# One head's exponential in seven units on GpSimd, in the forward attention of an adaLN transformer block

## The chip, the cores and the metric

The kernel runs on one core of one Trainium2 chip. The metric is the device time of one execution in microseconds (us). A core has five engines that run side by side and meet at semaphores: TensorE (PE, matrix products into PSUM), VectorE (DVE), ScalarE (ACT, here the exponentials), GpSimd (POOL) and SyncE (SP, which only issues DMAs). Each engine works through its own queue in order.

## The reference

The reference computes the output of one transformer block and all its gradients. The block has adaptive layer norms (shift, scale and gate from `silu(c) @ w_mod`), attention with 32 heads of 16 columns over 2048 tokens of width 512, and a squared-ReLU MLP of width 1792. All in bf16. The part that matters here is the attention of the forward pass:

```python
scores = jnp.einsum('bhqd,bhkd->bhqk', q, k) * Dh ** (-0.5)
p = _softmax(scores, axis=-1)
o = jnp.einsum('bhqk,bhkd->bhqd', p, v)
```

```python
h = _layernorm(x) * (1 + ca) + sa
x = x + ga * _A_ref(h, A_wqkv, A_wo)
...
_out, _vjp = jax.vjp(_f, A_x, A_wqkv, A_wo, B_w1, B_b1, B_w2, B_b2, c, w_mod)
```

## The kernel before

The kernel has four stages: a preparation (norm, first projections), the forward attention with the MLP and its gradients worked in between, the backward attention, and a tail of weight gradients. The change touches the forward attention alone.

**Units.** The forward attention is cut into 512 units `u`: four chunks of 512 queries (`qc`), in each of them eight head groups of four heads (`hg`), in each of them 16 tiles of 128 keys (`kt`). In the first query chunk unit `u` is key tile `u % 16` of head group `u // 16`. The loop runs `fscore(u)`, then `fpv(u - 2)`, then what is planned for unit `u`.

**Scores and exponentials.** `fscore` (L603 to L614) works in two pairs of heads. For each pair PE makes the scores of two heads, 128 keys by 512 queries each, in a PSUM tile `psST` of two banks; a row of `q` carries a bound on the row's maximum, so that no maximum has to be taken. ACT then takes the exponential of both heads at once, 1024 columns, into half of the SBUF tile `ET`, with the factor 0.25 of the scores in the same instruction (L614). There are three `psST` buffers, so 1.5 units.

**Products with V.** `fpv` (L616 to L630) multiplies the four heads' `ET` with `vaug` (V with a column of ones) into four row blocks of one PSUM tile `oacc`, which collects the 16 key tiles of a head group. At the last one DVE copies it to `ostage` (L632) and POOL casts that to `obf` (L640).

**Side work of the first chunk.** The remaining projections of the first stage are spread over its units by `plan_tasks`, an order written out by hand: key and query tiles (`key_tile`, L1050; `query_tile`, L1067; PE projects, DVE copies from PSUM, DVE squares the copy in `square`, L863), norms of them (`key_norm`: PE at L860, DVE's maximum at L857), an inverse square root in steps on DVE (`query_bound`, L1082 to L1093), rows of the modulation (L895, L897), columns of it (L885 to L888) and tiles turned to tokens (L1115, L1118, L1123). In units 83 to 110 DVE also normalizes and modulates tiles of x (L752 to L754), and from 113 on it forms gated gradients (L310). All PE products of this side work go through one PSUM buffer `pm` (pool `mm`, one buffer), which DVE empties. In a unit with no side product PE runs two products with zeros (`steady`, L657).

**POOL's queue.** POOL issues the row loads of the next head group (`fload`, `row_load`, L591): four of K rows, four of Q rows and one of the bounds, in the order of the program behind the `obf` cast of the last group. It also adds up row sums (`rowsum`, L168).

The queues of all engines are in program order (`manual_schedule`); the tile layer adds the semaphores.

Of the kernel before, what the change touches and what calls it, by code (L numbers as in the profile page):

```python
# [14 lines left out]
AF = mybir.ActivationFunctionType  # L15
ALU = mybir.AluOpType
AX = mybir.AxisListType
BF = dt.bfloat16
F32 = dt.float32

P = 128
# [3 lines left out]
DH = 16  # L25
HG = 8
FF = 1792
FC = 14
SCALE = 0.25
EPS = 1e-5  # L30
QPAD = 528


@with_exitstack
def kernel(
# [17 lines left out]
    PE = nc.tensor  # L53
    DVE = nc.vector
    ACT = nc.scalar
    POOL = nc.gpsimd
    SP = nc.sync

    persist = ctx.enter_context(tc.tile_pool(name="persist", bufs=1))
# [9 lines left out]
    DVE.memset(zeros[:], 0.0)  # L69
    onesf = persist.tile([P, 4], F32, name="onesf")  # L70
    DVE.memset(onesf[:], 1.0)
    modbc = persist.tile([P, 6, D], BF, name="modbc")
    modcol = persist.tile([P, 6, DC], F32, name="modcol")
    mean1 = persist.tile([P, TT], F32, name="mean1")
# [42 lines left out]
    def rsqrt_cols(pool, out, var, w):  # L117
        v, y, t = (pool.tile([P, w], F32, name=f"rsq{i}", tag=f"rsq{i}") for i in range(3))
        DVE.tensor_scalar(v[:], var, EPS, None, ALU.add)
        yi = y[:].bitcast(I32)  # L120
# [20 lines left out]
    vaug = vaugpool.tile([P, TT, H + 1, DH + 1], BF, name="vaug")  # L141
# [3 lines left out]
    with ExitStack() as ph:  # L145
        wk = ph.enter_context(tc.tile_pool(name="phC", bufs=2))
        ffw = ph.enter_context(tc.tile_pool(name="ffw", bufs=1))
        cb = ph.enter_context(tc.tile_pool(name="phMc", bufs=1))
# [29 lines left out]
        def later(lag, f, *args):  # L178
            due.append((unit[0] + lag, f, args, True))
# [407 lines left out]
        funits = [(qc, hg, kt) for qc in range(QC) for hg in range(HG) for kt in range(TT)]  # L587
# [5 lines left out]
        def fload(qc, hg):  # L593
# [6 lines left out]
            run_due()  # L600
            fh[qc, hg] = (qt_sb, kt_sb)

        def fscore(u):  # L603
            qc, hg, kt = funits[u]
            qt_sb, kt_sb = fh[qc, hg]
            ET = ework.tile([P, 4, 512], BF, name="ET", tag="ET")
            fe[u] = ET
            for pair in range(2):
                ps = pools["s"].tile([P, 2, 512], F32, name="psST", tag="psST")
                for hi in range(2):  # L610
                    r = 32 * (2 * pair + hi)
                    PE.matmul(ps[:, hi, :], kt_sb[r:r + 32, kt * P:(kt + 1) * P], qt_sb[r:r + 32, :],  # L612
                              start=True, stop=True, tile_position=(r, 0))
                ACT.activation(ET[:, 2 * pair:2 * pair + 2, :], ps[:], AF.Exp, scale=SCALE)  # L614

        def fpv(u):  # L616
            qc, hg, kt = funits[u]
            if kt == 0:
                fcur["o"] = pools["o"].tile([P, 512], F32, name="oacc", tag="oacc")
                if hg == 0:  # L620
                    fcur["rr"] = ework.tile([H, 512], F32, name="rrows", tag="rrows", bufs=1)
                    fcur["ou"] = ework.tile([P, 4, HG, P], BF, name="O_un", tag="O_un", bufs=1)
            oacc = fcur["o"]
            ET = fe.pop(u)
            for hq in range(4):
                h = hg * 4 + hq
                lhsT = vaug[:, kt].rearrange("p h c -> p (h c)")[:, h * (DH + 1):h * (DH + 1) + 32]
                PE.matmul(oacc[32 * hq:32 * hq + 32, :], lhsT, ET[:, hq, :],  # L628
                          start=(kt == 0), stop=(kt == TT - 1), tile_position=(0, 32 * hq), skip_group_check=True)
            if kt == TT - 1:  # L630
                ostage = ework.tile([P, 512], F32, name="ostage", tag="ostage", bufs=1)
                DVE.tensor_copy(ostage[:], oacc[:])  # L632
                obf = ework.tile([P, 512], BF, name="obf", tag="obf", bufs=2)
                if u == NF - 1:
                    fcur["last"] = ostage
                    return
                if hg == HG - 1:
                    DVE.tensor_copy(obf[:], ostage[:])
                else:
                    POOL.tensor_copy(obf[:], ostage[:])  # L640
                for hq in range(4):
                    h = hg * 4 + hq
                    later(2, sp, fcur["rr"][h:h + 1, :], ostage[32 * hq + 16:32 * hq + 17, :])
                later(3, sp, fcur["ou"][:, :, hg, :], obf[:], True)
                if hg == HG - 1:
                    fdone.append((u + 7, qc, fcur["rr"], fcur["ou"]))
# [252 lines left out]
        def prep():  # L899
# [19 lines left out]
            ACT.activation(tiny0[:], onesf[:, 0:1], AF.Sqrt)  # L919
            DVE.memset(epsc, EPS)  # L920
            DVE.memset(kmx, 0.0)
# [293 lines left out]
        with ExitStack() as ph2:  # L1215
# [3 lines left out]
            with tc.manual_schedule(engines={PE.engine, ACT.engine, DVE.engine, SP.engine, POOL.engine}):  # L1219
                fh[0, 0] = (qts[0], kts[0])  # L1220
                for u in range(NF + 2):
                    unit[0] = u
                    run_due()
                    if u < NF:
                        if funits[u][2] == (10 if u < 7 * TT else 2) and u + TT < NF:
                            fload(*funits[u + TT][0:2])
                        fscore(u)
                    begins = TT <= u - 2 < NF and funits[u - 2][2] == 0
                    if 2 <= u and not begins:
                        fpv(u - 2)  # L1230
# [15 lines left out]
                    if begins:  # L1246
                        fpv(u - 2)
# [55 lines left out]
        def last_chunk(O_c, L, w1T):  # L1303
# [29 lines left out]
            for half in range(2):  # L1333
# [12 lines left out]
                sd = wk.tile([P, 2], F32, name="sd2", tag="sd2")  # L1346
                DVE.tensor_scalar(sd[:], mv4[:, tis[0]:tis[1] + 1, 1], EPS, None, ALU.add)
                ACT.activation(sd[:], sd[:], AF.Sqrt)
# [170 lines left out]
            def ks_loads():  # L1519
                keep["KS"] = kpool.tile([P, TT, QPAD], BF, name="KS_tok", tag="ks")  # L1520
                POOL.memset(keep["KS"][:, :, D:QPAD], 0.0)
                for i in range(4):
                    later(1 + i, sp, keep["KS"][:, 4 * i:4 * i + 4, 0:D], k_st[:, 4 * i:4 * i + 4, :])
# [108 lines left out]
    with ExitStack() as ph:  # L1632
# [113 lines left out]
        def keep_warm():  # L1746
            PE.matmul(cur["vk"][0:DH, :], KS_tok[:, 0, D:QPAD], dOs_tok[:, 0, :], start=False, stop=False,
                      tile_position=(0, 0), skip_group_check=True)
# [79 lines left out]
        if True:  # L1828
# [4 lines left out]
            for b in range(NU // 4):  # L1833
                toks, bank = order_t if on_pe(b - 1) else order_n
                for tok in toks:
                    c, i = tok[0], int(tok[1:] or 0)
# [41 lines left out]
            late = (("dq", 1), ("vk", 4), ("dq", 2), ("vk", 5), ("dq", 3))  # L1878
# [367 lines left out]
```

## Time and profile before

| what | value |
|---|---|
| median of 3 runs | 2461.73 us (2460.39 to 2462.99) |
| the profiled execution | 2457.34 us, span 2455.5 us |
| first exponential of unit 0, last of unit 511 | 36.8 us, 978.5 us |
| first query chunk, 36.8 to 272.0 us | ACT busy 235.2, PE 222.5, DVE 122.5, POOL 51.0 us |
| busy in the whole span | PE 94%, ACT 93%, DVE 75%, POOL 20% |
| POOL's sum of 128x512 f32 tiles (L168 with g_c) | 1157 ns in the first chunk |
| DVE's copy of 128x512 f32 from PSUM (L632) | 687 ns |

Times in the profile are from one execution, counted from the start of its span. A line such as `L614 ACT ACTIVATE ET<-psST 128x1024 bf16<-128x1024 f32 x227 | 208.6, 1453 | 0.0` names the source line, the engine, the operation, what it writes and reads with shapes, how many there are, then busy us and mean ns of one, and the engine's idle time just before them with what ended it. A timeline line has start and duration in us first. Durations of ACT overlap, since an instruction is counted from when it enters the engine.

### The profile page before, as it was taken

The page shows a single profiled execution, that of the slowest core. Times are in us where ns is not written, and L with a number is a line of the kernel's source. Part 1 is how long each engine was busy: PE and PEld are TensorE (multiplying, and loading weights), DVE is VectorE, ACT ScalarE, POOL GpSimd, SP SyncE. Part 2 cuts the span into 40 slices and gives each one's busy share as a digit, 9 for nine tenths or more (in the row PEclk, how much of TensorE's full clock was granted, in tenths as well). Part 3 has the DMA queues.
Part 4 walks back from the last instruction along what each step waited for, and adds up shares of the span by engine and source line. Part 5 has one row for each costly group of instructions (what it writes and reads, how often), then busy time and mean ns, then how long its engine had stood idle before and what let it go on. Part 6 is the DMA issues. An engine that isn't in the chain of part 4 may idle for free. (4 is left out here: it accounts for less than half of the span.)

```text
span 2455.5 us, 49791 instructions
## 1 busy us (share of the span) xinstructions
PE 2307.4 (94%) x18926; PEld 774.3 (32%) x18926; DVE 1847.8 (75%) x2443; ACT 2295.4 (93%) x3579; POOL 500.1 (20%) x684
## 2 busy tenths in 40 slices
PE   8999899989998999889999999999999999999998
PEld 3232232333233323433333333233323233322243
DVE  6655464456445645679999999999999899999984
ACT  8999999999999999539999999999999999999964
POOL 2111224314542443110111101111011110110112
PEclk9999999999999999989999999999999899999999
DMA  4568445627683857879999999999999999999998
GB/s 155 138 158 188 110 113 120 170 68 125 99 178 62 139 81 165 223 191 193 206 206 201 204 203 208 205 207 204 206 208 210 203 204 209 203 203 199 204 209 171
DMA packets 1200324, 426.67 MB, mean 174 GB/s; under 512 B 1080758, under 2 KB 1177140, under 8 KB 1199956
## 3 DMA queue, kind: packets, MB, share of 16 engines
q1 hardware_dynamic: 1154900, 367.44, 79.7%
q0 software_dynamic: 23472, 33.77, 8.5%
q10 hardware_dynamic: 21712, 22.27, 3.8%
q8 instruction: 149, 2.44, 0.4%
q14 instruction: 91, 0.75, 0.1%
HBM read 85.46 MB, written 68.95 MB: 63 GB/s over the span
## 5 line engine op out<-in xcount | busy, mean ns | idle before, releaser
L1724 DVE TENSOR_TENSOR dS_u<-psD_u,E_u 128x1024 bf16<-128x1024 f32 x1024 | 1186.1, 1219 | 69.8 <-PE psD_u L1722 24.5
L614 ACT ACTIVATE ET<-psST 128x1024 bf16<-128x1024 f32 x1024 | 940.0, 1319 | 3.3 <-PE psST L612 3.3
L1708 ACT ACTIVATE E_u<-psS_A 128x512 bf16<-128x512 f32 x768 | 515.3, 671 | 15.4 <-DMA out_dram<-xlast 12.7
L1708 ACT ACTIVATE E_u<-psS_B 128x512 bf16<-128x512 f32 x768 | 507.9, 661 | 9.6 <-PE psD_u L1722 5.4
L1722 PE MATMUL psD_u<-iv,ido 32*128 32x512 bf16 x2048 | 408.8, 387 | 0.0
L612 PE MATMUL psST<-qt_sb,kt_sb 32*128 32x512 bf16 x2048 | 318.0, 382 | 41.2 <-ACT ET L614 38.0
L1708 ACT ACTIVATE E_u<-psS_C 128x512 bf16<-128x512 f32 x512 | 336.6, 657 | 2.3 <-PE psS_B L1702 0.8
L1702 PE MATMUL psS_A<-ik,iq 32*128 32x512 bf16 x768 | 293.0, 381 | 16.2 <-ACT E_u L1708 5.9
L1702 PE MATMUL psS_B<-ik,iq 32*128 32x512 bf16 x768 | 294.4, 383 | 7.9 <-ACT E_u L1708 0.2
L1809 POOL TENSOR_TENSOR dQacc<-dQacc,dqtmp 128x512 f32<-128x512 f32 x64 | 81.2, 1269 | 846.3 <-ACT dqtmp L1804 846.3
L1702 PEld LDWEIGHTS <-iq 32*128 32x128 bf16 x2048 | 130.1, 91 | 315.8 <-issue 299.7
L1764 PE MATMUL accVK<-dS_u,qz 128*32 128x512 bf16 x2048 | 212.8, 390 | 0.2 <-DVE dS_u L1724 0.2
L628 PE MATMUL oacc<-ET,vaug 128*32 128x512 bf16 x2048 | 206.6, 391 | 3.3 <-DVE ostage L632 3.3
L1773 PE MATMUL accVK<-E_u,dOs_tok 128*16 128x512 bf16 x2048 | 202.5, 385 | 0.0
L1702 PE MATMUL psS_C<-ik,iq 32*128 32x512 bf16 x512 | 194.2, 379 | 4.3 <-ACT dqtmp L1804 0.2
L612 PEld LDWEIGHTS <-kt_sb 32*128 32x128 bf16 x2048 | 89.6, 91 | 314.5 <-issue 290.1
L1791 PE MATMUL dqacc<-dsT,KS_tok 128*32 128x512 bf16 x2048 | 146.7, 384 | 18.4 <-DMA dsT<-dS_u 5.4
L1868 ACT ACTIVATE dsT<-ptT 128x1024 bf16<-128x1024 bf16 x126 | 145.0, 1150 | 3.1 <-PE ptT L1754 2.9
L1722 PEld LDWEIGHTS <-ido 32*128 32x128 bf16 x2048 | 104.5, 91 | 102.0 <-issue 95.6
L1764 PEld LDWEIGHTS <-qz 128*32 128x32 bf16 x2048 | 58.4, 94 | 177.3 <-issue 162.3
L252 DVE COPY part<-pm 128x512 f32<-128x512 f32 (+2 forms) x105 | 64.4, 614 | 63.5 <-PE pm L234 61.5
L324 DVE CAST dsT<-pm 128x512 bf16<-128x512 f32 x56 | 38.7, 691 | 84.9 <-PE pm L322 84.8
(435 smaller groups left out, 2700.6 us busy)
## 6 DMA issues: line engine op xcount, KB each, us to landing
p_st<-part POOLq DMA_DIRECT2D x36, 256.0 KB, 4.3
kt_sb<-qkT_st POOLq DMA_DIRECT2D x124, 64.0 KB, 3.9
wA<-in_B_w_dram SPq DMA_DIRECT2D x28, 256.0 KB, 5.8
w_nat<-in_B_w_dram SPq DMA_DIRECT2D x21, 256.0 KB, 4.7
w2T<-w2T_st SPq DMA_DIRECT2D x21, 256.0 KB, 5.5
p_st<-part POOLq DMA_DIRECT2D x27, 192.0 KB, 5.0
p_st<-part SPq DMA_DIRECT2D x18, 256.0 KB, 2.3
part<-p_st SPq DMA_DIRECT2D x18, 256.0 KB, 4.9
```

The costliest lines, as they stand in the source:

```text
L612: PE.matmul(ps[:, hi, :], kt_sb[r:r + 32, kt * P:(kt + 1) * P], qt_sb[r:r + 32, :], start=True, stop=True, tile_position=(r, 0))
L614: ACT.activation(ET[:, 2 * pair:2 * pair + 2, :], ps[:], AF.Exp, scale=SCALE)
L628: PE.matmul(oacc[32 * hq:32 * hq + 32, :], lhsT, ET[:, hq, :], start=(kt == 0), stop=(kt == TT - 1), tile_position=(0, 32 * hq), skip_grou ...
L1702: PE.matmul(psS[:], st["q"][r:r + 32, qt * P:(qt + 1) * P], st["k"][r:r + 32, kc * 512:kc * 512 + 512], start=True, stop=True, tile_positi ...
L1708: ACT.activation(bst[u][0][:, hq, :], sst.pop((u, hq))[:], AF.Exp, scale=SCALE)
L1722: PE.matmul(psD[:, hi, :], st["do"][r:r + 32, qt * P:(qt + 1) * P], st["v"][r:r + 32, kc * 512:kc * 512 + 512], start=True, stop=True, til ...
L1724: DVE.tensor_tensor(dS_u[:, 2 * pair:2 * pair + 2, :], psD[:], E_u[:, 2 * pair:2 * pair + 2, :], ALU.mult)
L1764: PE.matmul(cur["vk"][32 * hq:32 * hq + 32, :], hst[hg]["qz"][:, qt, hq, :], bst[u][1][:, hq, :], start=(qt == 0), stop=False, tile_positi ...
L1773: PE.matmul(acc[32 * hq:32 * hq + DH, :], dOs_tok[:, qt, (hg * 4 + hq) * DH:(hg * 4 + hq + 1) * DH], E_u[:, hq, :], start=False, stop=(qt ...
L1791: PE.matmul(acc[32 * hq:32 * hq + 32, :], KS_tok[:, kc * 4 + kt, h * DH:h * DH + 32], tT[:, :, hq * 4 + kt, :], start=(kt == 0), stop=(kt ...
L1809: POOL.tensor_tensor(dst2, dst, tmp[:], ALU.add)
L1868: ACT.activation(dst, pt[:], AF.Identity)
```

## The change

In the first query chunk, unit `16 * hg + 2` of the head groups 1 to 7 (units 18, 34, 50, 66, 82, 98 and 114) is treated in another way. Of its second pair of heads ACT takes the exponential of one head only, 512 columns. DVE multiplies the other head's scores by 0.25 log2(e) and puts them in SBUF as f32 (`staged`), and POOL raises 2 to them (`Epool`, bf16). POOL does this in one instruction of 512 columns for groups 1 to 3, in two of 256 for groups 4 and 5, and in four of 128 for groups 6 and 7. The product of that head with V is taken out of its own unit and done in the unit with `kt == 14` of the same group. `staged` and `Epool` take buffers of the tag `tk`, which is otherwise first used after this chunk.

In the built program the staging copy waits for ACT's half exponential of the same unit. On POOL the power stands behind the `obf` cast and ahead of the row loads of the next group; in group 7 one of these loads is ahead of it. In that group the staging copy stands between the first and the second of the gated gradients on DVE.

```diff
+LOG2E = 1.4426950408889634
...
+    twos = persist.tile([P, 1], F32, name="twos")
+    DVE.memset(twos[:], 2.0)
...
+        pooled = {16 * hg + 2: 512 // (1, 1, 1, 1, 2, 2, 4, 4)[hg] for hg in range(1, HG)}
+        owed = []
+
+        def on_pool(u, ET, scores):
+            staged = cb.tile([P, 512], F32, name="staged", tag="tk", bufs=5)
+            DVE.tensor_scalar(staged[:], scores, SCALE * LOG2E, None, ALU.mult)
+            out = cb.tile([P, 512], BF, name="Epool", tag="tk", bufs=5)
+            w = pooled[u]
+            for lo in range(0, 512, w):
+                POOL.tensor_tensor(out[:, lo:lo + w], twos[:].to_broadcast([P, w]), staged[:, lo:lo + w], ALU.pow)
+            owed.append((u, out))
+
         def fscore(u):
...
-                ACT.activation(ET[:, 2 * pair:2 * pair + 2, :], ps[:], AF.Exp, scale=SCALE)
+                if pair == 1 and u in pooled:
+                    ACT.activation(ET[:, 2, :], ps[:, 0, :], AF.Exp, scale=SCALE)
+                    on_pool(u, ET, ps[:, 1, :])
+                else:
+                    ACT.activation(ET[:, 2 * pair:2 * pair + 2, :], ps[:], AF.Exp, scale=SCALE)
 
         def fpv(u):
...
-            for hq in range(4):
+            parts = [(kt, hq, ET[:, hq, :]) for hq in range(3 if u in pooled else 4)]
+            if kt == 14 and owed:
+                v, late = owed.pop(0)
+                parts.append((funits[v][2], 3, late[:]))
+            for k, hq, rhs in parts:
                 h = hg * 4 + hq
-                lhsT = vaug[:, kt].rearrange("p h c -> p (h c)")[:, h * (DH + 1):h * (DH + 1) + 32]
-                PE.matmul(oacc[32 * hq:32 * hq + 32, :], lhsT, ET[:, hq, :],
+                lhsT = vaug[:, k].rearrange("p h c -> p (h c)")[:, h * (DH + 1):h * (DH + 1) + 32]
+                PE.matmul(oacc[32 * hq:32 * hq + 32, :], lhsT, rhs,
                           start=(kt == 0), stop=(kt == TT - 1), tile_position=(0, 32 * hq), skip_group_check=True)
```

## The prediction

> **What bounds the kernel now.** I read the page first: ACT is busy 93% of the span, PE 94%, and nearly all of the forty slices read 9 for ACT. The table by stage then shows the first query chunk alone, and the grouped lines of that stretch show what ACT does there.
>
> ```profile
> PE 2307.4 (94%) x18926; PEld 774.3 (32%) x18926; DVE 1847.8 (75%) x2443; ACT 2295.4 (93%) x3579; POOL 500.1 (20%) x684
> ...
> core 0: us, PE busy (x) PEld busy (x) DVE busy (x) ACT busy (x) POOL busy (x), PEclk, DMA share, GB/s
> 36.80:272.00 235.20, 222.53 (x1567) 70.94 (x1565) 122.51 (x246) 235.20 (x259) 50.97 (x97) 1.00 0.66 165
> ...
> L614 ACT ACTIVATE ET<-psST 128x1024 bf16<-128x1024 f32 x227 | 208.6, 1453 | 0.0
> ```
>
> ACT is busy for all 235.20 us of the chunk, with no idle time before any exponential. Its 256 exponentials of 1024 columns start 0.9165 us apart (the 1453 ns mean counts queueing), from 36.75 us on. So unit u needs its scores by 36.75 + 1.833u, and whatever makes ACT wait here lengthens the span one for one. PE computes scores about one unit ahead, and that lead is the only cushion. POOL is nearly free, DVE half busy.
>
> The timelines of DVE and PE around unit 34, a unit that the change touches, show how PE hangs on DVE:
>
> ```profile
> 99.37 0.68 DVE L857 TENSOR_REDUCE small<-pm 32x1 f32<-32x512 f32 x1
> 101.89 0.69 DVE L1050 CAST KT<-pm 128x512 bf16<-128x512 f32 x1 [1.83 <-PE pm L853]
> 102.61 0.43 DVE L863 TENSOR_TENSOR sqK<-KT 128x512 bf16<-128x512 bf16 x1
> ...
> 100.81 1.04 PE L853 MATMUL pm<-h1T,wqkv_nat 128*128 128x512 bf16 x4
> 101.78 0.60 PE L612 MATMUL psST<-qt_sb,kt_sb 32*128 32x512 bf16 x4
> 102.31 0.40 PE L628 MATMUL oacc<-ET,vaug 128*32 128x512 bf16 x4
> 103.09 0.38 PE L860 MATMUL pm<-sqK,small 128*32 128x512 bf16 x1 [0.38 <-DVE sqK L863]
> 103.31 0.59 PE L657 MATMUL oacc<-identb,zeros 128*16 128x512 bf16 x2
> 103.83 0.40 PE L612 MATMUL psST<-qt_sb,kt_sb 32*128 32x512 bf16 x4
> ```
>
> There is one `pm` buffer. PE's next side product waits until DVE has emptied it, and the next scores stand behind that product in PE's queue.
>
> Last, what an operation of POOL does to DVE (timeline of the second chunk, then one line's durations):
>
> ```profile
> 404.75 1.20 POOL L168 TENSOR_TENSOR racc<-racc,prod 128x512 f32<-128x512 f32 x1
> ...
> 405.33 0.91 DVE L505 TENSOR_TENSOR uqb<-dxn,tqb 128x512 bf16<-128x512 bf16 x1
> ...
> L505 DVE TENSOR_TENSOR uqb<-dxn,tqb x12: 415/774/909, 373.9 to 878.4; 128x512 bf16<-128x512 bf16 x12
> ...
> L1067 DVE CAST sP<-pm x15: 691/692/692, 72.5 to 182.6; 128x512 bf16<-128x512 f32 x15
> ```
>
> A DVE product of two SBUF tiles takes 0.415 us alone and 0.91 us when POOL's two-input sum is running: it ends 0.28 us after POOL's (404.75 + 1.20 = 405.95; 406.24). Evacuations of PSUM (L1067) never vary. So the DVE product waits out POOL's whole instruction.
>
> **What is saved.** In seven units ACT's second exponential has 512 columns instead of 1024. Exponentials of 512 columns (L1708, backward) start 0.48 us apart in the timeline, so 0.9165 - 0.48 = 0.44 us each, 3.1 us for seven. No more can be gained.
>
> **What moves at no cost.** Seven P·V products of 32 rows go from their unit to the one with kt = 14; a group of four starts within 0.01 us, and the fifth there costs at most one 0.2 us slot, covered by the filler products (L657). DVE's seven copies of PSUM to f32 (0.69 us, as the ostage copy L632) are 5 us of a half-busy engine.
>
> **POOL's queue.** The power stands ahead of the next group's nine row loads (0.5 us each to issue, 3.9 us to land). For group 4 they are needed at 153.0 us (PE's first scores of unit 64), and the power would start near 130.7. It may last 153.0 - 130.7 - 4.5 - 3.9 = 14 us before loads are late. The fourth head's product, due some 24 us after, comes later still.
>
> **The new wait.** DVE's staging copy waits for ACT's half exponential of its own unit, not just for PE's scores; that is how the built program orders the two readers of the score tile. ACT is about a unit behind PE, and DVE is in order: everything DVE owes PE queues behind. Unit 34: the half exponential starts at 36.75 + 69 x 0.9165 = 99.99, is done 0.6 us later (shortest L1708 row 0.592), and staging ends at 101.3. The reduction that ran at 99.37 runs at 101.3 to 102.0; PE's projection slips from 100.81 to 102.0; the scores of unit 36 follow 0.97 later, at 103.0, ready 0.38 later, at 103.4. ACT wants them at 102.74 - 0.44 = 102.3: 1.1 us idle, more than the 0.44 saved. The same sum gives 1.0 for unit 18 (70.05 reduction to 72.0, projection 71.47 to 72.65), 1.1 for unit 50 (L1082 from 129.17 to 130.6), about 1.5 for 66 (the same chain), 1.9 for 82 (DVE full), 0.8 for 98, 0 for 114 (filler products only): 7.4 us.
>
> **The power itself.** No row of before has one. The nearest is POOL's f32 sum of the same shape, 1.20 us, one pass: the lower end. A power needs a logarithm, a product and an exponential; the kernel's own inverse root (L1088 to L1093) takes six DVE passes. Four to twelve passes of 1.2 us give 4.8 to 14.4 us, an estimate. I take 5 us for 512 columns, since the sum is the only row of this engine and kind, and keep 1.2 and 14 for the range. The Trainium skill (GPSIMD Engine Reference, section Elementwise — side-by-side cycle accounting) puts data-dependent branching at about 12 cycles an element, which would be 5.1 us here and leave the sum where it is; no run shows it yet.
>
> **The ports.** If POOL holds DVE out as in L505, a power of 5 us stops DVE's next two-SBUF-input operation, and all that is queued behind it. Unit 34: the power runs 101.4 to 106.4; the projection's cast ends at 103.8; its square (L863) waits and ends at 106.7. The key norm (L860) needs that square, the scores of unit 37 come 0.74 later (103.09 to 103.83), ready at 107.8; ACT, by then 0.7 late, wants them at 104.57 + 0.7 = 105.2: 2.6 us more. Unit 18 (square 73.28 blocked to 77.0, reduction, key norm): 1.5. Unit 50 (L1088, which showed 0.70 for 0.44 beside POOL's cast, blocked to 135.7, the modulation row's cast behind it): 3.3. Unit 66, two pieces of 2.5 us: 1.9. Unit 82, two pieces in a DVE queue full of two-input work (L752 to L754) with the token copies behind: 4.9. Units 98 and 114, pieces of 1.25 us: about 0.2 and 0. Together 14.4 us, and about 5 us more or less for each us that the power differs from 5.
>
> The Trainium skill (SBUF — State Buffer, section Who interferes with whom) speaks against this change: the pair of ports that VectorE and GpSimd share is an exclusive lock held for a whole instruction, and a VectorE instruction with two SBUF inputs contends with a GpSimd one that reads SBUF. The trace agrees (0.91 against 0.415 us), though for no operation above 3 us; without that rule the sum would be 7.4 - 3.1 = +4.3 us.
>
> **Sum.** 7.4 + 14.4 - 3.1 = +18.7 us. The profiled execution, 2457.34 us (span 2455.5), becomes 2476. It lies 4.4 us under the median of the runs, 2461.73, and the sum goes on that: 2480.
>
> **Rivals.**
> 1. The power is cheap (under 3 us), or DVE gets the ports while POOL computes: only the new wait is left, +4 to +9 us, 2466 to 2471. For it: the one POOL row of this shape is 1.2 us. Against: a power is not one pass.
> 2. The power is long, over 9 us: +39 at 9, +64 at 14, and beyond 14 the loads are late as well: 2500 to 2530 and above. For it: the result is only asked for 14 units (26 us) later, so nothing in the program needs it short.
> 3. Not slower: PE's lead covers staging and blocked squares, and only the saving is left, -3.1 us, 2458.6. The price is 0.44 us a unit; it decides if PE's scores come at least 1.1 us earlier before need than I read. Against: PE's scores of unit 36 (101.78, ready 102.16) lead their need (102.74) by 0.6 us.
> 4. The change does less than it says, e.g. the half exponential costs as much as a whole one: +3 on top of any case; the 0.48 us spacing speaks against it.
>
> **How the numbers follow.** Forecast (power 3 to 9 us, ports held) 0.50; rival 2 0.26; rival 1 0.18; rival 3 0.06; rival 4 is inside their widths. About 0.2% of 2461.73, 4.9 us, is what a measurement of this kernel can tell from no change. Rival 1 lies half inside that (0.08), rival 3 nearly all (0.04), as even the full saving is only 3.1 us; 0.02 is left for faster. Slower: 0.50 + 0.26 + 0.10 = 0.86. Low end 2464: what a cheap power with a somewhat larger PE lead gives, leaving out 0.09. High end 2530: a power of 14 us, leaving out 0.10.
>
> **What would show it.** POOL's `Epool` rows: 5 us for 512 columns, about 2.5 and 1.3 for the pieces. DVE's `sqK`, `sqQ` or L1088 rows of several us beside them; `staged` with a wait on ACT; idle time of ACT before `ET`, released by PE, of about 22 us in all, in the units just after 18, 34, 50, 66 and 82; PE waiting for DVE's `small`, `sqK`, `rtv`. Everything after unit 114 only shifted. I am wrong if the blocked rows stay at 0.43 us, if ACT shows no idle time, or if most of the loss lies after the first chunk.

## The result, and the profile after

The changed kernel takes 2924.75 us (median of 4 runs, 2921.82 to 2936.16) against 2461.63 us before: 1.1875 times as long, 95% interval 1.1848 to 1.1902, so +463 us. The forecast was 2480, its range 2464 to 2530. The direction was right, the size was not. The profiled execution took 2936.16 us, its span is 2934.4, and it reads as follows.

The page first: shares of busy time, and three rows of the forty slices (73 us each).

```profile
PE 2322.1 (79%) x18853; PEld 778.8 (27%) x18926; DVE 1851.5 (63%) x2451; ACT 2298.3 (78%) x3579; POOL 1076.7 (37%) x699
...
ACT  8343124321999999999955999999999999999975
POOL 2988898899242144335301111101010101010112
PEclk9677567655999999999998999999999999999999
```

ACT's work is the same as before (2298 us against 2295), but its 9s are gone from slices 1 to 9 (counted from 0), and there, and nowhere else, POOL is full. POOL's busy time has grown by 577 us. So the loss lies in the first query chunk: from the first exponential of unit 0 to the last of unit 127 it now takes 633.6 us, before 234.8; another 66 us of idle time follow at once, at unit 128.

The timeline of POOL shows with what POOL is full (start, duration, engine, line, operation).

```profile
73.32 81.96 POOL L615 TENSOR_TENSOR Epool<-twos,staged 128x512 bf16<-128x512 f32 x1 [2.77 <-DVE staged L611]
155.26 2.01 POOL L594 DMA_DIRECT2D kt_sb<-qkT_st  x4
157.26 1.91 POOL L594 DMA_DIRECT2D qt_sb<-qkT_st  x4
159.16 0.57 POOL L594 DMA_DIRECT2D qt_sb<-m_st  x1
166.31 0.60 POOL L663 CAST obf<-ostage 128x512 bf16<-128x512 f32 x1 [6.57 <-DVE ostage L655]
169.07 81.96 POOL L615 TENSOR_TENSOR Epool<-twos,staged 128x512 bf16<-128x512 f32 x1 [2.16 <-DVE staged L611]
```

One power of 512 columns lasts 82 us, where I took 5. The nine row loads of the next head group are issued only when it is over; before, eight of the nine went out between 73.12 and 81.15 us, and the last at 90.41. The same place in ACT's, PE's and DVE's timelines:

```profile
160.93 0.71 PE L627 MATMUL psST<-qt_sb,kt_sb 32*128 32x512 bf16 x4 [64.76 <-DMA qt_sb<-m_st]
...
161.67 1.94 ACT L633 ACTIVATE ET<-psST 128x1024 bf16<-128x1024 f32 x2 [64.24 <-PE psST L627]
...
168.29 0.69 DVE L611 TENSOR_SCALAR staged<-psST 128x512 f32<-128x512 f32 x1 [0.85 <-ACT ET L630]
```

The brackets tell what ended the idle time: PE waited 64.76 us for the last row load, ACT 64.24 us for PE. These lines close a ring. Power 81.96 us; nine issues 4.5 (155.26 to 159.73); landing 1.2 (to 160.93); scores of unit 32 to the end of staging of unit 34, 8.1 (to 168.98). With 0.09 us to the next power these are the 95.75 us between the starts of the two powers (169.07 - 73.32). Before, a head group took 16 x 1.833 = 29.3 us. So each of seven groups loses about 66.4 us: 465 us, where 463 were measured. The list of waits from 36 to 760 us (total, times, longest) has nearly the same sum:

```profile
ACT ET L633 <- PE psST L627: 466.8, 28, 66.4
PEld L627 <- DMA qt_sb<-m_st: 457.8, 7, 67.2
```

Last, what I had expected to carry most of the loss: DVE operations with two SBUF inputs, held out while POOL computes. DVE's timeline, inside the first power (73.32 to 155.28):

```profile
75.66 0.43 DVE L886 TENSOR_TENSOR sqQ<-sP 128x512 bf16<-128x512 bf16 x1
...
82.51 0.42 DVE L886 TENSOR_TENSOR sqK<-KT 128x512 bf16<-128x512 bf16 x1
```

And the line's durations in the whole run (min/median/max ns, first and last start):

```profile
L886 DVE TENSOR_TENSOR sqK<-KT x16: 403/424/427, 61.7 to 193.5; 128x512 bf16<-128x512 bf16 x16
```

None of these is held. The squares take what they took before (402 to 427 ns), in the middle of an 82 us instruction that reads SBUF. What is held is an operation that comes right behind a power's start, and only for a moment. POOL's and DVE's timelines of group 5, whose power is in two pieces of 256 columns:

```profile
457.23 82.24 POOL L615 TENSOR_TENSOR Epool<-twos,staged 128x256 bf16<-128x256 f32 x2 [2.29 <-DVE staged L611]
...
457.33 0.79 DVE L1112 TENSOR_SCALAR rty<-rty 32x512 int32<-32x512 int32 x1
```

The DVE operation, from SBUF to SBUF, takes 0.40 us elsewhere; here it ends 0.88 us after the power began, and the next ones, 40 us before the piece is over, take 0.40 and 0.42 again.

### The profile page after: what moved, and what is told of

It is laid out like the page before. It is cut to its first block, busy times and chain, and to the rows that moved or that the text cites. A ratio compares the mean times of both kernels' runs of the same rounds, so it can differ in the third digit from the quotient of the medians.

```text
span 2934.4 us, 49746 instructions
## 1 busy us (share of the span) xinstructions
PE 2322.1 (79%) x18853; PEld 778.8 (27%) x18926; DVE 1851.5 (63%) x2451; ACT 2298.3 (78%) x3579; POOL 1076.7 (37%) x699
## 5 line engine op out<-in xcount | busy, mean ns | idle before, releaser
L627 PE MATMUL psST<-qt_sb,kt_sb 32*128 32x512 bf16 x2048 | 309.3, 390 | 490.9 <-DMA qt_sb<-m_st 454.4
L615 POOL TENSOR_TENSOR Epool<-twos,staged 128x128 bf16<-128x128 f32 (+2 forms) x15 | 576.0, 38411 | 15.6 <-DVE staged L611 11.3
L1832 POOL TENSOR_TENSOR dQst<-dQacc,dqtmp 128x512 bf16<-128x512 f32 x32 | 40.7, 1271 | 263.5 <-ACT dqtmp L1827 263.5
```

The costliest lines, as they stand in the source:

```text
L615: POOL.tensor_tensor(out[:, lo:lo + w], twos[:].to_broadcast([P, w]), staged[:, lo:lo + w], ALU.pow)
```

## The experiments

**Theory (queue).** The whole loss is the length of the power, 0.160 us a column, in POOL's in-order queue: loads, and behind them the product with V, come late. The ports play no part. **Rivals:** the ports of DVE and POOL; the new wait of `staged` for ACT's half exponential (my 7.4 us); the product with V that needs `Epool` in the same group. Diffs are against the changed kernel unless something else is said.

### A product in place of the power

```diff
-                POOL.tensor_tensor(out[:, lo:lo + w], twos[:].to_broadcast([P, w]), staged[:, lo:lo + w], ALU.pow)
+                POOL.tensor_tensor(out[:, lo:lo + w], twos[:].to_broadcast([P, w]), staged[:, lo:lo + w], ALU.mult)
```

> The power is replaced by a product of the same operands and shapes (so the fourth head of these seven units is not an exponential). POOL then spends about 1.2 us per unit (its f32 sums of this shape took 1.16 to 1.27), as I had allowed for rival 1. If the wait of the staging copy for ACT costs what I worked out (7.4 us of idle ACT, less 3.1 saved), the run is +4 to +6 us against before; if that wait is covered by PE's lead, -3 us; if what is slow in the change is anything but the power's own duration (the wait, the moved products, the buffers), several hundred us remain.

Measured: 2461.09 us (12 runs), ratio 0.9991 (0.9973 to 1.0009). All but a few us of the 463 hang on that one word. POOL's rows, with the same operands and tiles:

```profile
L615 POOL TENSOR_TENSOR Epool<-twos,staged x15: 390/570/1036, 73.3 to 257.4; 128x128 bf16<-128x128 f32 x8, 128x256 bf16<-128x256 f32 x4, 128x512 bf16<-128x512 f32 x3
```

1.036 us for 512 columns where the power takes 82: 79 times. What is left of the change is now visible. ACT loses time after the six units that I had named. It is counted here from the ends of the exponentials, as what lies between two ends beyond the usual 0.9165 us (0.48 for a half); the forecast of the new wait stands in brackets: after 18, 1.1 us (1.0); 34, 1.2 (1.1); 50, 1.4 (1.1); 66, 2.3 (1.5); 82, 2.5 (1.9); 98, 0.7 (0.8); 114, none (0). That is 9.2 us, where I had 7.4. (The profile's list of waits has 7.4 us for the same stretch, since it counts only the time in which ACT holds no instruction at all. Idle times of ACT in a chunk are counted by ends from here on.) The first chunk takes 241.0 us against 234.8: +6.3, about 9.2 less the 3.1 saved. Not all of the 9.2 need be the new wait: the product itself holds four DVE operations, by 0.2 to 0.4 us each.

The whole run does not show the +6.3: its interval is -6.6 to +2.2 us, so some of it must come back later. Where was not found. The stages behind the forward attention last 1462 to 1488 us in single profiles of kernels that do not differ there, so a few us cannot be followed to the end.

The operation shown above inside the power is held by this product too:

```profile
195.06 1.36 POOL L615 TENSOR_TENSOR Epool<-twos,staged 128x256 bf16<-128x256 f32 x2 [2.59 <-DVE staged L611]
195.16 0.79 DVE L1112 TENSOR_SCALAR rty<-rty 32x512 int32<-32x512 int32 x1
```

It starts 0.10 us behind POOL in both kernels and takes 0.79 us in both, though POOL's instruction of 256 columns lasts 0.61 us here and 41.15 there. In the two kernels of the next section it takes 0.47 us behind a power of 64 columns and 0.58 behind one of 128. So a power does hold DVE, but only at its start, and as far as these few rows go for no longer than a product of as many columns would.

### The power on 64 and on 128 columns

The power on the first columns only, the product on the rest (here 64; the second kernel has 128 and 384):

```diff
-            for lo in range(0, 512, w):
-                POOL.tensor_tensor(out[:, lo:lo + w], ..., staged[:, lo:lo + w], ALU.pow)
+            POOL.tensor_tensor(out[:, 0:64], ..., staged[:, 0:64], ALU.pow)
+            POOL.tensor_tensor(out[:, 64:512], ..., staged[:, 64:512], ALU.mult)
```

> Only 64 of the 512 columns are raised by the power (the other 448 are a product, so not an exponential), one instruction each. At 160 ns a column the power takes 10.3 us and both together 11.4. Theory queue (the row loads behind the power are late only when POOL is held for more than 14 us): nothing but the staging wait, +4 to +6 us. Theory ports (POOL holds out the two-input operations of DVE for as long as it runs): about +50 us, with DVE's squares at up to 10 us.

> 128 of the 512 columns are raised by the power (the other 384 are a product, so not an exponential). Power 20.6 us, both together 21.5. Theory queue: each unit is late by 21.5 - 14 = 7.5 us less what ACT has in hand, about 5 us a unit, +30 to +50 us. If the product with V were what waits (due some 23 us after the power starts), only the staging wait is left, +4 to +6. Theory ports: about +118 us.

Measured: with 64 columns 2461.78 us, ratio 0.9997 (0.9979 to 1.0015); with 128 columns 2501.42, ratio 1.0156 (1.0125 to 1.0187), +31 to +46. The powers take 10.55 and 20.76 us; with the product behind them POOL is held for 11.5 and 21.6 us. Between the two lies the margin of 14 us that I had read for the loads. (With 66.4 us lost to a power of 82 it is nearer 82 - 66.4 = 15.6: the last load landed 1.2 us after its issue in the changed kernel, where I had counted 3.9.) Below it ACT idles 8.3 us in the chunk, no more than with the product; above it some 46 us up to unit 128, 3.3 to 5.3 of them at each of units 32, 48, 64, 80, 96, 112 and 128, the first units that use late loads, and up to 1.9 in the unit after. If a power held the ports to its end, 10.55 us of it would have cost some 40 us by my ports step.

The second kernel also shows power and product side by side. Here are DVE's square and POOL's product that met, in the timeline:

```profile
129.10 1.11 DVE L886 TENSOR_TENSOR sqK<-KT 128x512 bf16<-128x512 bf16 x1
...
129.11 0.82 POOL L615 TENSOR_TENSOR Epool<-twos,staged 128x384 bf16<-128x384 f32 x1
```

The square takes 1.11 us instead of 0.42 and ends 0.28 us after the product (129.93, 130.21), as in the row of before. The squares inside the 20.76 us power take 0.42.

### Row loads on another queue

```diff
-            POOL.dma_start(out=to, in_=fro)
+            (SP if unit[0] < 128 else POOL).dma_start(out=to, in_=fro)
```

> As the changed kernel, but the row loads of the first chunk are issued by SP, so none of them stands behind the power. Theory queue alone: if the loads were the only thing that waits for POOL, only the staging wait is left, +5 us. Theory result: the fourth head's product with V, due about 23 us after the power starts, is next in line and waits 82 - 23 = 59 us per unit, +410 us; so taking the loads off POOL would give back only some 50 of the 463 us.

Measured: 2877.32 us, ratio 1.168 (1.1628 to 1.1732). Only 47 us come back. The loads are in time, ACT no longer idles at unit 32, but 59 us at unit 33, 49, 65 and so on. The list of waits names the next in line:

```profile
ACT ET L633 <- PE psST L627: 421.2, 26, 61.1
PE oacc L651 <- POOL Epool L615: 404.3, 7, 60.1
```

PE stands at the product with V of the fourth head, due 24 us after the power starts: 82 - 24 = 58 us, seven times that is 406, and the list has 404.3. That was the step I had put behind the loads ("comes later still").

### Row loads on another queue, without the fourth head's product

The same, and the product of those seven heads' `Epool` with V is left out:

```diff
-            if kt == 14 and owed:
+            if kt == 14 and owed and False:
```

> The power stays; the row loads of the first chunk are issued by SP, and the fourth head's product with V is left out in the seven units. Theory that only those two wait for POOL: +5 us, the staging wait. Theory capacity: POOL has 7 x 82 = 574 us of powers in a chunk of 235 us, its casts of the group results and the chunk's row sums queue behind them, and the first chunk cannot be finished before POOL is: +300 to +350 us.

Measured: 2811.48 us, ratio 1.141 (1.1377 to 1.1443), +347. With nobody waiting for the result POOL is still the bound, its timeline having no gap:

```profile
72.24 81.96 POOL L615 TENSOR_TENSOR Epool<-twos,staged 128x512 bf16<-128x512 f32 x1 [2.77 <-DVE staged L611]
154.18 0.60 POOL L663 CAST obf<-ostage 128x512 bf16<-128x512 f32 x1
154.76 81.92 POOL L615 TENSOR_TENSOR Epool<-twos,staged 128x512 bf16<-128x512 f32 x1
236.64 0.60 POOL L663 CAST obf<-ostage 128x512 bf16<-128x512 f32 x1
237.21 81.91 POOL L615 TENSOR_TENSOR Epool<-twos,staged 128x512 bf16<-128x512 f32 x1
```

The way to ACT is now a third one. SP, which issues the loads, first has to send `obf` off, and POOL's cast of `obf` stands behind a power (the list of waits):

```profile
SPq L179 <- POOL obf L663: 328.6, 6, 63.5
```

So moving the loads or the product makes no room: 7 x 82 = 574 us of POOL do not fit into a chunk of 235 us.

### Long products in place of the power

Three products of 1536 columns each, 8.5 us of POOL in every one of the seven units:

```diff
-            out = cb.tile([P, 512], BF, name="Epool", tag="tk", bufs=5)
-            ...
+            out3 = cb.tile([P, 3, 512], BF, name="Epool", tag="tk", bufs=5)
+            for _ in range(3):
+                POOL.tensor_tensor(out3[:], <twos, broadcast>, <staged, three times>, ALU.mult)
+            out = out3[:, 0, :]
```

> The power is replaced by three products of the same two operands, each over 1536 columns (the operands repeated; not an exponential), about 2.9 us each, 8.7 in all, which is less than the 10.5 us of the power on 64 columns. Theory that any POOL instruction reading SBUF holds out DVE's two-input and SBUF-to-SBUF operations until it ends: several DVE rows of the lines that took 0.40 to 0.43 us beside the power now take 1 to 3.3 us, ACT idles about 7 us more than in the run with one product, +12 us. Theory that the broadcast operand or this tile is what keeps the ports free: rows stay at 0.43, +5 us.

Measured: 2478.97 us, ratio 1.0064 (1.0043 to 1.0084), +11 to +21. The first chunk takes 258.3 us, 17.2 more than with the short product, and ACT idles 26.3 us instead of 9.2: 17 more, where 7 were expected. POOL's rows (min/median/max ns of one product):

```profile
L614 POOL TENSOR_TENSOR Epool<-twos,staged x21: 2742/2754/2852, 72.8 to 278.5; 128x1536 bf16<-128x1536 f32 x21
```

DVE's squares and modulations, the same columns:

```profile
L886 DVE TENSOR_TENSOR sqK<-KT x16: 402/425/2460, 61.2 to 129.5; 128x512 bf16<-128x512 bf16 x16
...
L776 DVE TENSOR_TENSOR tmpT<-tmpT,modbc x16: 424/426/2928, 210.1 to 254.7; 128x512 bf16<-128x512 bf16 x16
```

A square of 2.46 us, a modulation of 2.93 us: the mechanism of my ports step exists, for products. With the power in the same place and ten times as long, both lines stay at 403 to 427 ns.

### The power on fewer rows

The product over the whole tile, then the power on 64 columns of r rows:

```diff
+            POOL.tensor_tensor(out[:], twos[:].to_broadcast([P, 512]), staged[:], ALU.mult)
+            r = {18: 128, 34: 64, 50: 32, 66: 16, 82: 8, 98: 4, 114: 1}[u]
+            POOL.tensor_tensor(out[0:r, 0:64], twos[0:r].to_broadcast([r, 64]), staged[0:r, 0:64], ALU.pow)
```

> The fourth head of the seven units gets the product over all its rows and columns, and then a power on 64 columns of only some of the rows: 128, 64, 32, 16, 8, 4 and 1 row for groups 1 to 7 (the weights that result are not exponentials). It asks what the 10.55 us of a power of 64 columns hang on. Theory 'a column at a time': all rows of a column go together, so each power lasts 10.55 us, whatever the number of rows. Rival 'element by element over all rows': 10.6, 5.3, 2.6, 1.3, 0.7, 0.4, 0.2 us. Rival 'the rows are shared out to equal workers, each of which takes its own one after the other': 10.55 us down to the rows of one worker, and in proportion below that. The power now starts about 1 us later and is over at most 11.6 us after staging, under the 14 us of the row loads, so all three expect no idle time of ACT at units 32, 48, ... and a time like that of the kernel before, within the spread of single runs (2450 to 2475 us).

Measured: 2470.12 us (one run). POOL's timeline:

```profile
73.25 10.75 POOL L616 TENSOR_TENSOR Epool<-twos,staged 128x64 bf16<-128x64 f32 x1
...
163.77 10.62 POOL L616 TENSOR_TENSOR Epool<-twos,staged 16x64 bf16<-16x64 f32 x1
...
256.48 10.62 POOL L616 TENSOR_TENSOR Epool<-twos,staged 1x64 bf16<-1x64 f32 x1
```

One row costs what 128 cost. The price hangs on the columns alone, 0.165 to 0.168 us each here, and nothing is won by cutting the tile the other way.

### The same relief on DVE

Against the kernel before: DVE forms one head's exponential itself, as the bits of a bf16 number, with one linear function into int16 (an approximation of the exponential); POOL has no part in it.

```diff
+                if pair == 1 and u in [16 * hg + 2 for hg in range(1, HG)]:
+                    DVE.tensor_scalar(ET[:, 3, :].bitcast(dt.int16), ps[:, 1, :], SCALE * 1.4426950408889634 * 128, (127 - 0.0562) * 128, ALU.mult, ALU.add)
+                    ACT.activation(ET[:, 2, :], ps[:, 0, :], AF.Exp, scale=SCALE)
```

> The same seven heads, but DVE makes the exponential itself, in one operation from PSUM, as bf16 bits (a linear function of the score rounded to int16, about 3% off at most), ahead of ACT's half exponential in the order, so DVE waits for nothing but PE; POOL and the late product are gone. Theory that the staging wait for ACT is what made ACT idle: ACT idles 1 to 2 us in the chunk instead of 9, the chunk is some 1 to 2 us shorter than before, and the whole run the same within the error. If the copy's time on DVE were what costs, the idle time would stay near 9 us.

Measured: 2459.6 us (10 runs), ratio 0.9984 (0.9964 to 1.0004). The chunk falls from 234.8 to 233.2 us, half of the 3.1 saved, and ACT loses 1.5 us where it lost 9.2: as the first theory has it, the order behind ACT was what cost, and not the 0.69 us on DVE (POOL's share is gone here as well). The whole run cannot tell. Then the same in every third and in every second unit of chunks two to four, where PE waits 28 us for ACT and spends 29 us on products with zeros:

> The kernel before with one head's exponential taken by DVE as bf16 bits (one linear function into int16, 0.69 us), now in every third unit of the second to fourth chunk (128 units) and in none of the first. Theory 'ACT binds there, PE has slack': before, PE waits 28 us for ACT in these three chunks and spends 29 us more on products with zeros; each such unit saves ACT 0.9165 - 0.48 = 0.44 us, 56 us in all; half of it or more arrives: the stretch from the first chunk's end to the last exponential falls from 708 to about 660 to 685 us, and the run by 20 to 45 us, 2415 to 2440. Rival 'PE binds as soon as ACT does not': scores and side products arrive no earlier, ACT sits idle before exponentials (released by PE) for what it saved, and the run stays within 8 us of the kernel before.

> The same in every second unit of these chunks (192 units). Theory 'ACT binds there, PE has slack': 84 us less work for ACT; the gain is larger than with every third unit until the 28 + 29 us of PE's slack are used up: 30 to 57 us, 2405 to 2430. Rival 'PE binds as soon as ACT does not': the same time as with every third unit, within 8 us of the kernel before, or slower, because DVE's 0.69 us stands ahead of the side work's evacuations and PE waits for its one pm buffer.

Measured: 2465.73 us, ratio 1.0026 (1.0008 to 1.0045), and 2477.03 us, ratio 1.0084 (1.0055 to 1.0114): slower, and more so with more of it. The first theory fails, and the rival named the wrong culprit. The lists of waits (272 to 990 us) of the kernels with a third and with a half of the units:

```profile
ACT ET L616 <- DVE ET L615: 38.5, 40, 2.4
ACT ET L618 <- PE psST L612: 16.1, 41, 2.2
```

```profile
ACT ET L616 <- DVE ET L615: 69.0, 73, 2.1
ACT ET L618 <- PE psST L612: 14.9, 40, 1.2
```

ACT's half exponential stands behind DVE's half of the same unit, and DVE, in order, comes to it late. These lists have 54.6 us of waits against 56 saved, and 84 against 84, but again they hold only the time in which ACT is empty. Counted by the ends of the exponentials, ACT loses 65 and 97 us more than before in these three chunks, so they take 717.5 and 721.7 us against 708.5 in the profiles. By the medians the runs are 7 and 18 us slower; how these sizes come out of 9 and 13 was not taken apart. The order of two readers of one score tile is paid either way: DVE behind ACT in the changed kernel, ACT behind DVE here. Nothing that was run is measurably faster than the kernel before.

### The kernel before once more

> The kernel before, unchanged, for a second profile of it. First chunk 234.8 us again (256 exponentials 0.9165 us apart); the backward stage, which moves most of the bytes, may differ by some us from the first profile. If it does, a loss of about 6 us in the first chunk, as in the profile with the product, can be lost in a comparison of whole runs.

Measured: 2471.94 us in one run. Its stretches up to the last exponential agree with the first profile of before within 1 us (chunk 234.8 and 234.8, chunks two to four 709.3 and 708.5); what follows takes 1488 us against 1475. In these two profiles the difference comes from there.

## Why the prediction was right or wrong, step by step

- **What is saved.** 0.44 us a unit. Right: in units 82, 98 and 114 of the kernel with the product, where nothing waits right behind the half exponential, the next one starts 0.478 us after it, against 0.9165.
- **What moves at no cost.** Nothing contradicts it: with the product in POOL's place nobody waits for `Epool`, and the lost time lies right behind the changed units, where the new wait was expected. It was not tested by itself.
- **POOL's queue.** Right in kind: 11.5 us on POOL pass, 21.6 do not, and 14 lies between (15.6 by the loss in the changed kernel).
- **The new wait.** Right in place and nearly in size: 9.2 us against 7.4, some of it from the product that stood in for the power. With the order turned round (the relief on DVE) 1.5 us are left.
- **The power itself. The step that failed:** "I take 5 us for 512 columns", with 14 kept as the upper end. It is 81.96 us. I had one POOL row, the sum at 1.20 us, and counted passes of it, by the pattern of DVE's inverse root. That is no bound: the power took 79 times as long as a product of the same operands, where I had four to twelve passes. Why was not tried. The sum for the right price was written down: beyond 14 us the loads are late, and 82 - 14 = 68 us in each of seven groups is 476 us, against 463. That the late loads are the path is shown: with the loads on SP, the next thing behind the power takes over. The mechanism stood in the text as rival 2 (0.26), but priced only as far as 14 us; "2530 and above" left the rest without a number. The figure of the Trainium skill (GPSIMD Engine Reference, Elementwise — side-by-side cycle accounting) that I had set beside my 5 us, about 12 cycles an element for data-dependent branching, gives 5.1 us, an estimate, if a column of 128 rows is one element. The trace has 16 times as much. Whether the page means an element so, no run shows.
- **The ports. A second step that failed.** 14.4 us forecast, three quarters of the sum, and for a power next to nothing found: one of my signs of being wrong, "if the blocked rows stay at 0.43 us", came true. I carried the behaviour of POOL's sum over to an operation that no row showed. For products it holds, but my sizes were too large there too: 8.5 us of products cost 17.2 us, where the rule of 5 us more or less per us gives about 14.4 + 5 x 3.5 = 32. The Trainium skill (SBUF — State Buffer, Who interferes with whom) makes the lock hold for any GpSimd instruction that reads SBUF, and for its whole length; the products agree (2.46 and 2.93 us beside 2.74), the power does not (0.42 beside 82). What the power does is hold DVE in its first moments: the operation that starts 0.10 us behind it ends 0.56, 0.67 and 0.88 us after the start of 64, 128 and 256 columns, the last as behind a product of 256. That would fit a power that reads all its input first and computes from then on; this was not tried and stays open.
- **The rivals.** Rival 1 (the new wait alone) is what the product and the 64 column power did inside the chunk, +6.3 and +5.6 us. Rival 3 is out, since PE's lead did not cover the new wait (9.2 us); rival 4 is out by the 0.478 us.

## What to carry to other kernels

An operation that no row of the trace shows on this engine has no price, and a count of passes of another operation is not an upper bound: time it alone first, on 64 columns, or carry the forecast through to prices ten and a hundred times as high. What stands behind it in the engine's queue sets how long it may be (here some 14 to 16 us), and once the engine's total is over the stage's length (574 us in 235), no re-ordering helps. When two engines read one tile of scores, look at which of them the built program lets go first: with the product on POOL and in the two kernels with many units on DVE, the wait cost more than the shared work saved.

## What the runs showed of the hardware

- A power of f32 to bf16 on GpSimd takes 0.160 to 0.168 us a column (10.55 to 10.75 us for 64, 20.7 for 128, 41.1 for 256, 81.96 for 512), and on 64 columns as much for 1 row as for 128; the product of the same operands takes 1.036 us for 512 columns.
- In the middle of a power DVE's products of two SBUF tiles run undisturbed (403 to 427 ns). An operation of DVE from SBUF to SBUF that starts 0.10 us after a power is held, for about as long as a product of as many columns would hold it (0.79 us behind 256 columns of either, 0.40 without). During a product of POOL they wait for its end and finish 0.28 us later.
- The granted clock fell where PE starved: 0.65 and 0.66 in the stretches of 73 to 162 and 162 to 258 us (PE busy 22 of 89 and 28 of 96 us), 1.00 in the same chunk before. It can be only a small part of the 8.1 us in the ring above: from the first exponential of unit 32 to the end of staging of unit 34 it is 7.3 us there and 6.2 with the product in place of the power, 1.1 more with the clock and all else. The rest of the ring is POOL's power and the loads.
